# Which of three PSUM banks the soft-max may use, and when the first float16 attention tiles are given out

## The chip, the cores and the metric

The kernel runs on one core of a Trainium2 chip. A core has TensorE (PE, matrix products, with its weight loads shown apart as PEld), VectorE (DVE), ScalarE (ACT), GpSimd (POOL) and SyncE (SP), which here only issues transfers. Each works through its own list of instructions in order, and semaphores make one wait for another. PE writes into PSUM banks, which DVE and ACT read. The metric is the device time of one execution in microseconds (us); smaller is better.

## The reference

Attention within chunks of 64 positions, then a mixture layer with squared ReLU, then a soft mixture over 32 slots. Cut to what matters:

```python
scores = scale * q_c @ k_c^T            # 8 batches, 8 heads, 9 chunks of 64 x 64
attn = softmax(scores, axis=-1)
x = (attn @ v_c) -> rows                # 4608 tokens x 512
h = maximum(x @ w_in, 0.0)              # 512 -> 2048
x = (h * h) @ w_out                     # 2048 -> 512
logits = x @ phi                        # 4608 x 32
d = softmax over the tokens (axis 0);  slot_input = d.T @ x
slot_out[e] = maximum(slot_input[e] @ w1[e], 0.0) @ w2[e]      # 8 experts
out = softmax over the slots (axis 1) of logits @ slot_out
```

## The kernel before, in words

**Tiles and blocks.** The tokens are cut into 36 attention tiles of 128 rows. Tiles 0 to 8 are computed in float32 (`attention32`), tiles 9 to 35 as pairs of float16 values (`attention`). Tiles are grouped into blocks of three (the first two blocks are smaller). For a block, the squared-ReLU layer runs as 16 steps, one for each 128 of the 2048 hidden columns: a step is 12 matmuls into the buffer `hps` (line 780), a ReLU and a square on ACT, and for most steps a transpose `gT` on PE (815) that ACT copies away (213). After the 16 steps of block b the generator `soft(b)` updates a running soft-max over all tokens, one stage to a step: the logits `L` are scaled to `Ls` (980), PE spreads them into a bank `l4` (990), DVE takes the maximum (1000, 1001) and ACT the exponential `dts` (1004), PE turns the logits (949) and the exponentials (1018), and PE multiplies the exponentials by the hidden values into `y` (1068), which DVE adds to `acc` (1052).

**One float16 tile, in order.** `total` (207: largest values), `flip`, `top`, `spread`, `scale` (420, 425, 429, 240: one scale for v), `reduce`, `finish` (230, 240, 243: scales for q and k), `hi` on ACT (446), `lo` on DVE (451), the transposing DMA `T` into `qkT` (472), `qd` (476), the scores `qk` on PE (487 to 489), `max` and `less` on DVE (493, 496), `exp` on ACT (502), `sums` on DVE (507 to 509), `normal` on POOL (512), `phi` on ACT (522), `plo` on POOL (525), the transposing DMA `PT` into `pT` (528), `pv` on PE (539 to 541), `xh` (545), `xl` (551). Parallel to it `vh` on POOL (461) and `vl` on DVE (466) fill `vbd`. Buffers go by the parity of the tile number; those of the first float16 tiles are made anew (`zero`, 181 and 182) once the float32 tile of the same parity has done its `pv` (708).

**What sets the order.** Up to the end of the float32 tiles a planner (`list_schedule`) writes the order out. After that a loop over steps t does, in each step: it gives out the operations of the tiles that are due (`put_until`, `put`), then the step's 12 matmuls, ReLU and square, then the stages of the soft-max that are due, then the transpose of the step two before. Each operation of a tile has a stage number, which is compared with the step (`FIRST` for tiles 9 to 11, `STAGES` from tile `FULL` = 12 on). `put` holds one back until what it depends on has been given out, and by `behind` some steps earlier: at least one step for PE behind another engine, two or three behind a DMA. From step `ALL_FROM` = 23 on the code's order holds on PE, DVE, ACT and POOL; before that only on PE, and a scheduler orders the others.

**The banks.** Three PSUM banks, `misc0` to `misc2`, serve all of the small PE work: `reduce`, `flip`, `spread`, `qk`, `pv` and the soft-max. `misc()` gives them out in turn and passes over a bank that is in `held_banks`: there a tile's operation is entered, when it is given out, with the operations that read it (`gives`), and it stays until these are given out too. The soft-max calls `misc()` without such an entry. Whoever writes into a bank waits, by semaphore, until those who read its last contents are done.

Of the kernel before, what the change touches and what calls it, by code (L numbers as in the profile page):

```python
# [20 lines left out]
P = 128  # L21
# [19 lines left out]
FULL = 12  # L41
# [44 lines left out]
def kernel(  # L86
# [25 lines left out]
    dve, act, pool, pe, sp = nc.vector, nc.scalar, nc.gpsimd, nc.tensor, nc.sync  # L112
# [77 lines left out]
    ps_h = ps1.enter_context(tc.tile_pool(name="ps_h", bufs=2, space=PSUM))  # L190
    ps_m = ps1.enter_context(tc.tile_pool(name="ps_m", bufs=1, space=PSUM))
    bank_of, n_misc, turn, held_banks = {}, [0], [None], {}

    def misc():
        x = bank_of.get(turn[0])
        if x is None:
            while n_misc[0] % 3 in held_banks:
                n_misc[0] += 1
            x = n_misc[0] % 3
            n_misc[0] += 1  # L200
            if turn[0] is not None:
                bank_of[turn[0]] = x
        return ps_m.tile([P, 512], F32, tag=f"misc{x}", name="misc")
# [734 lines left out]
    def late_keep(x, eng):  # L938
        moe_keep(NB - 1, NF - LATE + x, eng)
# [35 lines left out]
    def soft(b):  # L975
        nonlocal cmat
        s0, n = blocks[NB if b == 1 else b]
        L, iv = L_ps.pop(b), iv2_all[:, s0 : s0 + n]
        Ls = big.tile([P, 4, P], F32, tag="Ls", name="Ls")[:, :n]
        dve.tensor_tensor(  # L980
            out=Ls, in0=L[:, : n * P].rearrange("p (j t) -> p j t", j=n),
            in1=iv.unsqueeze(2).to_broadcast([P, n, P]), op=ALU.mult,
        )
        if b == 2:
            second_gT[0] = True
        yield
        if cmat is None:
            cmat = const.tile([P, NT, NS], F32, tag="lg", name="cmat", bufs=1)
        l4 = misc()[:, : n * P]
        pe.matmul(  # L990
            l4, sel4.rearrange("p a s -> p (a s)"), Ls.rearrange("p j t -> p (j t)"),
            start=True, stop=True,
        )
        yield
        rm = sm.tile([P, 1], F32, tag="rm", name="rm", bufs=2)
        nm = sm.tile([P, 1], F32, tag="nm", name="nm", bufs=2)
        al = sm.tile([P, 1], F32, tag="al", name="al", bufs=2)
        rsum = sm.tile([P, 1], F32, tag="rsum", name="rsum", bufs=2)
        dts = big.tile([P, 4, P], F32, tag="dts", name="dts")[:, :n]
        dve.tensor_reduce(out=rm, in_=l4, axis=AX.X, op=ALU.max)  # L1000
        dve.scalar_tensor_tensor(
            out=nm, in0=rm, scalar=-1.0, in1=run_n, op0=ALU.mult, op1=ALU.min
        )
        act.activation(  # L1004
            out=dts.rearrange("p j t -> p (j t)"), in_=l4, func=ACTF.Exp, bias=nm, accum_out=rsum
        )
        act.activation(out=al, in_=run_n, func=ACTF.Exp, bias=nm, scale=-1.0)
        dve.tensor_copy(run_n, nm)
        yield
        new_sum(al, rsum)  # L1010
        cs = slots_exp(s0, n, slots_turn(Ls, n, misc()))
        if b > 2:
            yield
        slots_share(s0, n, cs)
        yield
        tp = misc()[:, : n * NS].rearrange("p (j s) -> p j s", s=NS)
        for j in range(n):
            pe.transpose(tp[:, j], dts[:NS, j], ident[:NS, :NS])
        dd = wk.tile([P, 3, NS], F32, tag="dd", name="dd", bufs=1)[:, :n]
        parts = None  # L1020
        if b in BY_DMA:
            top, inv = (sm.tile([P, w], F32, tag=f"iv{w}", name="iv", bufs=2) for w in (1, 3))
            dve.tensor_reduce(out=top, in_=iv, axis=AX.X, op=ALU.max)
            dve.reciprocal(inv[:, :1], top)
            dve.tensor_scalar(inv, iv, inv[:, :1], 8.0, ALU.mult, ALU.mult)
            pool.tensor_scalar(
                out=top, in0=top, scalar1=0.125, scalar2=1.0, op0=ALU.mult, op1=ALU.mult
            )
            act.activation(out=acc, in_=acc, func=ACTF.Copy, scale=al)
            iv = inv  # L1030
        dve.tensor_tensor(  # L1031
            out=dd, in0=tp, in1=iv.unsqueeze(2).to_broadcast([P, n, NS]), op=ALU.mult
        )
        if b in BY_DMA:
            parts = aux_of()[1].rearrange("p (l j s) -> p l j s", l=6, j=3)[:, 3 * (b % 2) : 3 * (b % 2) + 3]
            dve.tensor_scalar_mul(parts[:, 0], dd, 4096.0)
            dve.scalar_tensor_tensor(
                out=parts[:, 1], in0=dd, scalar=4096.0, in1=parts[:, 0],
                op0=ALU.mult, op1=ALU.subtract,
            )  # L1040
            dve.tensor_scalar_mul(parts[:, 2], parts[:, 0], 2.0 ** -12)
        if b > 2:
            yield
        y = misc()
        for j in range(n):
            slot_sums(b, y, dd, j, n, parts)
        if b in BY_DMA:
            dve.scalar_tensor_tensor(
                out=acc, in0=y, scalar=top, in1=acc, op0=ALU.mult, op1=ALU.add
            )  # L1050
        else:
            dve.scalar_tensor_tensor(
                out=acc, in0=acc, scalar=al, in1=y, op0=ALU.mult, op1=ALU.add
            )
        yield
# [253 lines left out]
    convs = {f: conv(f) for f in range(NF)}  # L1309
    emitted = set()  # L1310

    def emit(task, name, op):
        emitted.add((task, name))
        turn[0] = (task, name)
        op()
        turn[0] = None
        if (task, name) in bank_of:
            held_banks[bank_of[task, name]] = [(task, n) for n in gives[name]]
        for x, users in list(held_banks.items()):
            if all(u in emitted for u in users):  # L1320
                del held_banks[x]


    fa, fb = PARTS
# [218 lines left out]
    for i in range(9, NT):  # L1543
        b, j = tile_block[i]
# [7 lines left out]
    def behind(t, op, d):  # L1552

        eng = tiles[d[0][1]][d[1]].eng if d[0][0] == "t" else ""
        gap = (3 if op.eng == "pe" else 2) if eng == "dma" else op.eng == "pe" and eng != "pe"
        return t - placed.get(d, -99) >= gap

    def put(i, stage, t):
        whole = True
        for n, op in tiles[i].items():  # L1560
            me = ("t", i)
            if op.stage <= stage and (me, n) not in emitted:
                full = len(held_banks) == 3 and op.eng == "pe"
                if not full and all(
                    d in emitted and behind(t, op, d)
                    for d in (d if isinstance(d, tuple) else (me, d) for d in op.deps)
                ):
                    placed[me, n] = t
                    emit(me, n, op)
                else:  # L1570
                    whole = False
        return whole
# [58 lines left out]
    t = min(0, min(slots, default=0))  # L1631
# [2 lines left out]
    )  # L1634
    while t < end or any(x >= t for x in slots):
        if t == ALL_FROM:
            ctx.enter_context(
                tc.manual_schedule(engines={getattr(mybir.EngineType, e) for e in ALL})
            )
        put_rest(t)  # L1640
        put_until(t + 1)
        b, f = steps[t] if 0 <= t < len(steps) else (None, None)
        if b == 2 and f % QF == 0:
            put_rest(t, [("s", NB, x) for x in range(f, f + QF)])
        if b is not None:
            end_step = (b, f) == (NB - 1, NF - 1)
            moe_h(b, f)
            moe_relu(b, f)
            if end_step:
                late_turn(0)  # L1650
                late_keep(0, "dve")
            if by_dma(b, f):
                moe_parts(b, f)
            else:
                moe_square(b, f)
            if (b, f) == (NB - 1, NF - 1):
                give((big, f"xb{b % 2}", 1536))
        if 1 <= t <= len(steps) and by_dma(*steps[t - 1]):
            moe_rest(*steps[t - 1])
        for fn in slots.pop(t, []):  # L1660
            fn()
        if b == NB - 1 and f % 2:
            give((big, f"wi{f // 2}", 1024))
        if 0 <= t - LAG < len(steps):
            b, f = steps[t - LAG]
            if (b, f) < (NB - 1, NF - LATE) and not by_dma(b, f):
                moe_turn(b, f)
                moe_keep(b, f)
            if f % QF == QF - 1 and (b, f) != (NB - 1, NF - 1):
                moe_logits(b, f // QF)  # L1670
            if f == NF - 1:
                if b < NB - 1:
                    run_gen(t + 1, soft(b))
                else:
                    soft_last()
        t += 1
# [212 lines left out]
```

## Time and profile before

| | |
|---|---|
| median of 3 runs | 775.44 us (771.95 to 776.62) |
| the profiled execution | 771.75 us |
| its span, first to last instruction | 770.0 us |
| PE busy in the span | 694.6 us, 90% |
| DVE, ACT, POOL busy | 499.5, 467.7, 196.8 us |
| mean granted clock of PE | 0.976 of full speed |

A busy share says how long an engine had work under way. An engine that is busy throughout sets the time; where it idles, the row of its wait tells who released it. The page also cuts the span into 40 slices of 19.25 us.

### The profile page before, as it was taken

The numbers are of one execution on the slowest core, as the hardware profiler recorded it, in microseconds if no ns is written. First come the engines' busy times: TensorE is split into PE (matmuls) and PEld (weight loads), VectorE is DVE, ScalarE is ACT, GpSimd is POOL, SyncE is SP. The second block draws the span as 40 slices with busy tenths as digits, with TensorE's granted clock in tenths as the row PEclk, the third lists the DMA queues.
The fourth block names the chain that finished last, engine by engine and source line by source line (L and its number), as shares of the span: only waits on it lengthen the run. The fifth ranks groups of instructions, "written<-read, shape, count | busy, mean of one in ns | idle before, by whom it ended". The sixth has DMA issues, their size and how long they took to land.

```text
span 770.0 us, 16709 instructions
## 1 busy us (share of the span) xinstructions
PE 694.6 (90%) x6491; PEld 437.8 (57%) x6491; DVE 499.5 (65%) x1108; ACT 467.7 (61%) x954; POOL 196.8 (26%) x250
## 2 busy tenths in 40 slices
PE   4688999888399899999999999999999999999983
PEld 3577776655256556555565565655655656553342
DVE  4899996256644778887778787777877741123134
ACT  3688887663446567667576675766766765541133
POOL 3222211122213335444333132232322310002010
PEclk9899999999799999999999999999999999999988
DMA  7796833214605746678577686785776976478979
GB/s 156 218 268 175 219 122 123 52 36 107 137 15 97 124 101 126 123 132 155 104 128 124 122 160 115 135 129 105 152 124 129 244 213 184 131 286 333 385 262 345
DMA packets 280655, 123.06 MB, mean 160 GB/s; under 512 B 251648, under 2 KB 268032, under 8 KB 280576
## 3 DMA queue, kind: packets, MB, share of 16 engines
q1 hardware_dynamic: 280576, 122.00, 66.8%
q8 instruction: 51, 0.84, 0.5%
q14 instruction: 28, 0.23, 0.1%
HBM read 78.71 MB, written 9.44 MB: 114 GB/s over the span
## 4 chain that ended last, share of the span: by engine, by line
PE 64%; DVE 19%; DMA 8%; ACT 3%; issue 3%; POOL 1%; SPq 1%; DVEq 0%; POOLq 0%; ACTq 0%
PE hps L780 36%; PE gT L815 4%; PE misc L1068 4%; PE L L866 4%; DMA qkv<-in_q_dram 3%; DMA qkv<-in_v_dram 2%; DVE qk L301 2%; DVE am L207 2%; PE ehps L1720 2%; DVE vbd L466 2%; DVE parts L847 1%; DVE qk L451 1%; DMA unit<-in_moe_w_dram 1%; DMA qkT<-qk 1%; PE misc L487 1%
## 5 line engine op out<-in xcount | busy, mean ns | idle before, releaser
L780 PE MATMUL hps<-xb,wi 128*128 128x384 f16 (+2 forms) x2400 | 409.6, 321 | 0.0
L780 PEld LDWEIGHTS <-wi 128*128 128x128 f16 x2400 | 222.3, 98 | 141.0 <-issue 20.1
L796 ACT ACTIVATE g<-hps 128x384 f32<-128x384 f32 x144 | 70.8, 491 | 125.7 <-PE hps L780 125.1
L803 ACT ACTIVATE g<-g 128x384 f32<-128x384 f32 (+2 forms) x188 | 96.9, 515 | 5.2
L213 ACT ACTIVATE G<-gT 128x384 f32<-128x384 f32 (+2 forms) x128 | 58.8, 459 | 23.5 <-PE gT L815 12.4
L207 DVE TENSOR_REDUCE am<-qkv 128x1 bf16<-128x512 f32 x90 | 59.1, 678 | 19.5 <-DMA qkv<-in_v_dram 11.3
L815 PE MATMUL gT<-ident,g 128*128 128x128 f32 x372 | 63.8, 278 | 2.5 <-ACT G L213 2.5
L525 POOL TENSOR_TENSOR p<-ex,p 128x512 f16<-128x512 f32 x27 | 34.3, 1271 | 116.4 <-ACT p L522 116.4
L815 PEld LDWEIGHTS gT<-ident,g 128*128 128x128 f32 x372 | 46.3, 143 | 20.7 <-issue 9.8
L461 POOL TENSOR_SCALAR vbd<-qkv,avs 64x512 f16<-64x512 f32 x54 | 47.0, 871 | 39.7 <-DVE vbd L181 20.1
L466 DVE SCALAR_TENSOR_TENSOR vbd<-qkv,avs,vbd 64x512 f16<-64x512 f32 x54 | 45.7, 846 | 2.9 <-POOL vbd L461 2.1
L796 ACT ACTIVATE g<-hps,inv_w 128x384 f32<-128x384 f32 (+2 forms) x56 | 29.9, 533 | 27.3 <-PE hps L780 25.5
L451 DVE SCALAR_TENSOR_TENSOR qk<-qkv,as,qk 128x512 f16<-128x512 f32 x54 | 44.8, 869 | 0.8 <-ACT qk L446 0.8
L248 POOL TENSOR_SCALAR iv_all<-avi 128x1 f32<-128x1 f32 x27 | 14.7, 544 | 111.5 <-DVE avi L243 109.4
L866 PE MATMUL L<-g,wp 128*32 128x384 f32 x384 | 41.9, 498 | 0.0
L512 POOL TENSOR_TENSOR ex<-ex,rs 128x512 f32<-128x512 f32 x27 | 30.6, 1133 | 40.8 <-DVE es L439 15.6
L847 DVE SCALAR_TENSOR_TENSOR parts<-parts,g 128x384 f16<-128x384 f16 x64 | 35.7, 557 | 7.3 <-ACT g L803 6.6
L446 ACT ACTIVATE qk<-qkv,as 128x512 f16<-128x512 f32 x54 | 35.7, 709 | 4.1 <-DVE as L240 4.1
L841 ACT ACTIVATE parts<-g 128x384 f16<-128x384 f32 x64 | 33.5, 523 | 2.0
L1068 PE MATMUL misc<-G,dd 128*32 128x512 f32 x180 | 33.5, 596 | 1.1 <-DVE dd L1031 1.1
L487 PE MATMUL misc<-qkT,qbd 128*128 128x64 f16 x216 | 21.9, 194 | 13.4 <-ACT dts L1004 13.4
L539 PE MATMUL misc<-pT,vbd 128*128 128x64 f16 x216 | 22.3, 195 | 10.5 <-DMA pT<-p 10.5
(213 smaller groups left out, 1166.5 us busy)
## 6 DMA issues: line engine op xcount, KB each, us to landing
unit<-in_moe_w_dram SPq DMA_DIRECT2D x49, 512.0 KB, 6.5
qkv<-in_q_dram SPq DMA_DIRECT2D x72, 128.0 KB, 3.2
qkv<-in_k_dram SPq DMA_DIRECT2D x72, 128.0 KB, 3.5
qkv<-in_v_dram SPq DMA_DIRECT2D x72, 128.0 KB, 3.4
stage<-in_moe_w_in_dram SPq DMA_DIRECT2D x16, 512.0 KB, 5.1
stage<-in_moe_w_out_dram SPq DMA_DIRECT2D x16, 512.0 KB, 6.2
unit<-in_moe_w_dram SPq DMA_DIRECT2D x27, 256.0 KB, 6.9
out_dram<-o SPq DMA_DIRECT2D x20, 256.0 KB, 2.8
```

The costliest lines, as they stand in the source:

```text
L207: dve.tensor_reduce(out=am, in_=src, axis=AX.X, op=ALU.max, apply_absolute_value=True)
L213: act.activation(out=out, in_=in_, func=ACTF.Copy)
L451: dve.scalar_tensor_tensor(out=qk16[:, 2 * a + 1], in0=flat[:, a], scalar=v["s"][:, a : a + 1], in1=qk16[:, 2 * a], op0=ALU.mult, op1=ALU. ...
L461: pool.tensor_scalar(out=dst[0], in0=vin, scalar1=v["sv"][pr], scalar2=1.0, op0=ALU.mult, op1=ALU.mult,)
L466: dve.scalar_tensor_tensor(out=dst[1], in0=vin, scalar=v["sv"][pr], in1=dst[0], op0=ALU.mult, op1=ALU.subtract,)
L780: pe.matmul(hp, wi[f][:, wl, kt], xb[:, xl, kt], start=(nm == 0), stop=(nm == 3 * KT - 1))
L796: act.activation(out=g, in_=hp, func=ACTF.Relu, scale=sc)
L803: act.activation(out=g, in_=g, func=ACTF.Square)
L815: pe.transpose(gt_ps[b, f][:, j], g[:, j * P : (j + 1) * P], ident)
L847: dve.scalar_tensor_tensor(out=part[:, 1], in0=part[:, 0], scalar=-4096.0, in1=g, op0=ALU.mult, op1=ALU.add)
L866: pe.matmul(L_ps[g0][NS * x : NS * x + NS, :n], wp[:, QF * q + x], g[:, x, :n], start=(q == 0), stop=(q == NQ - 1), tile_position=(0, NS * x),
L1068: pe.matmul(y[NS * g : NS * g + NS], lhs, rhs, start=(j == 0 and x == 0), stop=(j == n - 1 and last), tile_position=(0, NS * g), skip_grou ...
```

## The change

There are three edits.

1. A bank taken for the soft-max's `l4` is entered in `held_banks` under the name ("soft", b), and `let_go` takes it out after the stage that reads it has been written (`keep`). This holds from step 23 on.
2. From step 23 on `misc()` gives out, of the banks that are not held, the one that was taken or let go longest ago, in place of the next in turn.
3. In `put`, tiles below `FULL` (9 to 11) no longer ask `behind`, nor whether all three banks are held: what they depend on must have been given out, and their stage number must have come.

```diff
-    def misc():
+    last_use, by_age = {0: 0, 1: 0, 2: 0}, [False]
+
+    def used(x):
+        n_misc[0] += 1
+        last_use[x] = n_misc[0]
+
+    def misc(keep=None):
         x = bank_of.get(turn[0])
-        if x is None:
-            while n_misc[0] % 3 in held_banks:
+        if x is None and by_age[0]:
+            x = min((y for y in last_use if y not in held_banks), key=last_use.get)
+            used(x)
+            if turn[0] is not None:
+                bank_of[turn[0]] = x
+            if keep is not None:
+                held_banks[x] = [keep]
+        elif x is None:
+            while len(held_banks) < 3 and n_misc[0] % 3 in held_banks:
                 n_misc[0] += 1
...
-        l4 = misc()[:, : n * P]
+        l4 = misc(("soft", b))[:, : n * P]
...
         dve.tensor_copy(run_n, nm)
+        let_go(("soft", b))
         yield
...
+    def let_go(*done):
+        emitted.update(done)
+        for x, users in list(held_banks.items()):
+            if all(u in emitted for u in users):
+                del held_banks[x]
+                if by_age[0]:
+                    used(x)
...
-                full = len(held_banks) == 3 and op.eng == "pe"
+                full = len(held_banks) == 3 and op.eng == "pe" and i >= FULL
                 if not full and all(
-                    d in emitted and behind(t, op, d)
+                    d in emitted and (i < FULL or behind(t, op, d))
...
         if t == ALL_FROM:
+            by_age[0] = True
```

The instructions are the same in kind and number. The lines of the changed kernel lie 12 or 13 lower (487 becomes 499, 949 becomes 961).

**Place 1: the first float16 scores.** PE, behind the last float32 `pv` (708, then 720), before:

```order
L708 MATMUL misc<-pT,vbd 64x64 x16
L420 LDWEIGHTS am
L420 MATMUL misc<-aux,am 1x128
L780 LDWEIGHTS wi_1780
L780 MATMUL hps<-xb_86,wi_1780 128x384
```

And there in the changed kernel:

```order
L720 MATMUL misc<-pT,vbd 64x64 x16
L499 LDWEIGHTS qbd
L499 MATMUL misc<-qkT,qbd 128x64
L500 LDWEIGHTS qbd
L500 MATMUL misc<-qkT,qbd 128x64
L501 LDWEIGHTS qbd
L501 MATMUL misc<-qkT,qbd 128x64
...
L432 LDWEIGHTS am
L432 MATMUL misc<-aux,am 1x128
```

The 24 matmuls of tile 9's scores now stand directly behind that `pv`; before, three steps of 12 matmuls lay between. Its `pv` moves up by one step.

**Place 2: tile 9's way to its `pT`.** ACT between the exponential of tile 9's scores (`ex_83`) and its `phi` (`p_85`), before:

```order
L502 ACTIVATE ex_83<-ex_83,es 128x512
L796 ACTIVATE g<-hps,inv_w 128x384
L213 ACTIVATE G<-gT 128x3x128
L803 ACTIVATE g<-g 128x384
...
L213 ACTIVATE G<-gT 128x3x128
L446 ACTIVATE qk_80<-qkv_78,as 128x512 x2
L1004 ACTIVATE dts,rsum<-misc,nm 128x384
L522 ACTIVATE p_85<-ex_83 128x512
```

In the changed kernel:

```order
L514 ACTIVATE ex_83<-ex_83,es 128x512
L808 ACTIVATE g<-hps,inv_w 128x384
L225 ACTIVATE G<-gT 128x3x128
L815 ACTIVATE g<-g 128x384
L808 ACTIVATE g<-hps,inv_w 128x384
L225 ACTIVATE G<-gT 128x3x128
L534 ACTIVATE p_85<-ex_83 128x512
L815 ACTIVATE g<-g 128x384
L458 ACTIVATE qk_81<-qkv_79,as 128x512 x2
```

SP there, before (`p_85` is tile 9's, `p_84` tile 10's):

```order
L391 DMA qkv_79<-in_q_dram 64x8x64 x2
L472 DMA_TRANSPOSE qkT<-qk_81 128x16x128
L391 DMA qkv_79<-in_k_dram 64x8x64 x2
L391 DMA qkv_78<-in_q_dram 64x8x64 x2
L472 DMA_TRANSPOSE qkT<-qk_80 128x16x128
L528 DMA_TRANSPOSE pT<-p_85 128x8x128
L528 DMA_TRANSPOSE pT<-p_84 128x8x128
```

In the changed kernel:

```order
L403 DMA qkv_78<-in_v_dram 64x8x64 x2
L540 DMA_TRANSPOSE pT<-p_85 128x8x128
L403 DMA qkv_79<-in_q_dram 64x8x64
L484 DMA_TRANSPOSE qkT<-qk_81 128x16x128
L403 DMA qkv_79<-in_q_dram 64x8x64
L403 DMA qkv_79<-in_k_dram 64x8x64 x2
L540 DMA_TRANSPOSE pT<-p_84 128x8x128
```

On both engines tile 9's step now stands ahead of the `hi` and the `T` of tile 11 (and, on SP, of tile 12's), behind which it stood before.

**Place 3: the scores behind a soft-max bank.** PE at step 45, tile 17, with the engines each waits for, before:

```order
L420 MATMUL misc_4065<-aux_2066,am_3698 1x128 [waits DVE_49]
L487 LDWEIGHTS qbd_2317 [waits DMAHW6_49,DVE_49]
L487 MATMUL misc_4069<-qkT_2319,qbd_2317 128x64 [waits Activation_49]
L488 LDWEIGHTS qbd_2317
...
L780 MATMUL hps_4097<-xb1_87,wi2_920 128x384
L949 MATMUL misc_4113<-sel1_67,Ls_3969 128x32 [waits DVE_49]
```

In the changed kernel:

```order
L432 MATMUL misc_4065<-aux_1994,am_3698 1x128 [waits DVE_49]
L499 LDWEIGHTS qbd_2317 [waits DMAHW6_49,DVE_49]
L499 MATMUL misc_4069<-qkT_2319,qbd_2317 128x64 [waits DVE_49]
L500 LDWEIGHTS qbd_2317
...
L792 MATMUL hps_4097<-xb1_87,wi2_920 128x384 [waits Activation_49]
L961 MATMUL misc_4113<-sel1_67,Ls_3969 128x32 [waits Activation_49]
```

No instruction moves here: the scores got another bank, and the soft-max's own bank goes to its next matmuls (949), behind the step's 12.

## Rows read from the trace of the kernel before

**Rows 1.** The page: busy time of PE; granted clock in 40 slices, tenths

```profile
PE 694.6 (90%) x6491; PEld 437.8 (57%) x6491; DVE 499.5 (65%) x1108; ACT 467.7 (61%) x954; POOL 196.8 (26%) x250
PEclk9899999999799999999999999999999999999988
```

**Rows 2.** One stretch: length, then PE, PEld, DVE, ACT, POOL busy; clock; DMA

```profile
308.00:385.00 77.00, 73.42 (x693) 44.68 (x691) 62.01 (x145) 51.16 (x104) 31.77 (x37) 1.00 0.70 129
```

**Rows 3.** Waits of PE, 154 to 280 us: total, times, longest

```profile
PE misc L539 <- DMA pT<-p: 10.5, 1, 10.5
PE misc L429 <- DVE xb L719: 2.7, 1, 2.7
PE misc L487 <- ACT dts L1004: 2.7, 1, 2.7
PE misc L230 <- DVE ex L496: 1.3, 1, 1.3
```

**Rows 4.** Waits of PE, 280 to 640 us

```profile
PE misc L487 <- ACT dts L1004: 10.7, 6, 1.8
```

**Rows 5.** Timeline of PE, 160 to 235 us: start, length, instruction

```profile
175.80 1.15 PE L708 MATMUL misc<-pT,vbd 128*64 128x64 f32 x32
...
187.73 0.20 PE L487 MATMUL misc<-qkT,qbd 128*128 128x64 f16 x1
...
209.05 0.21 PE L539 MATMUL misc<-pT,vbd 128*128 128x64 f16 x1 [10.53 <-DMA pT<-p]
...
210.42 0.18 PE L429 MATMUL misc<-tm,ones 1*128 1x1 bf16 x1
...
210.58 3.98 PE L780 MATMUL hps<-xb,wi 128*128 128x384 f16 x12
```

**Rows 6.** Timeline of PE, 255 to 270 us

```profile
264.62 0.19 PE L487 MATMUL misc<-qkT,qbd 128*128 128x64 f16 x1 [2.68 <-ACT dts L1004]
...
265.32 3.77 PE L780 MATMUL hps<-xb,wi 128*128 128x384 f16 x12
```

**Rows 7.** Timeline of PE, 305 to 322 us

```profile
315.78 0.19 PE L487 MATMUL misc<-qkT,qbd 128*128 128x64 f16 x1 [1.79 <-ACT dts L1004]
...
316.48 2.11 PE L780 MATMUL hps<-xb,wi 128*128 128x384 f16 x12
```

**Rows 8.** Timeline of all engines, 196 to 206 us

```profile
196.76 1.04 POOL L512 TENSOR_TENSOR ex<-ex,rs 128x512 f32<-128x512 f32 x1 [8.03 <-ACT ex L502]
...
198.41 1.34 ACT L446 ACTIVATE qk<-qkv,as 128x512 f16<-128x512 f32 x2 [1.31 <-DVE as L240]
...
200.21 0.62 ACT L522 ACTIVATE p<-ex 128x512 f16<-128x512 f32 x1
200.28 2.32 DVE L451 SCALAR_TENSOR_TENSOR qk<-qkv,as,qk 128x512 f16<-128x512 f32 x2
...
200.90 1.15 POOL L525 TENSOR_TENSOR p<-ex,p 128x512 f16<-128x512 f32 x1 [3.10 <-ACT p L522]
...
202.66 2.88 SPq L472 DMA_TRANSPOSE qkT<-qk  x1
...
205.64 1.25 SPq L528 DMA_TRANSPOSE pT<-p  x1
```

**Rows 9.** Timeline of DVE, 150 to 212 us

```profile
174.83 0.86 DVE L476 COPY qbd<-qkT 64x1024 f16<-64x1024 f16 x2 [2.37 <-DMA qkT<-qk]
175.70 0.75 DVE L1052 SCALAR_TENSOR_TENSOR acc<-acc,al,misc 128x512 f32<-128x512 f32 x1
...
182.02 2.46 DVE L207 TENSOR_REDUCE am<-qkv 128x1 bf16<-128x512 f32 x4
```

**Rows 10.** Line 451 in the whole trace: shortest, median, longest in ns

```profile
L451 DVE SCALAR_TENSOR_TENSOR qk<-qkv,as,qk x54: 699/751/1655, 167.9 to 601.1; 128x512 f16<-128x512 f32 x54
```

**Rows 11.** Timeline of all engines, 313 to 318 us

```profile
313.18 0.15 DVE L243 TENSOR_SCALAR ai<-misc 128x2 int32<-128x2 int32 x1
...
315.06 0.58 ACT L1004 ACTIVATE dts<-misc,nm 128x384 f32<-128x384 f32 x1
```

More of the change, by code (lines that the diff above doesn't have):

```diff
@@ L1318, in emit @@
             held_banks[bank_of[task, name]] = [(task, n) for n in gives[name]]
-        for x, users in list(held_banks.items()):
-            if all(u in emitted for u in users):
-                del held_banks[x]
+        let_go()
     fa, fb = PARTS
```

## The prediction

> **What bounds the kernel now.** I read the page first, then stretches of 77 us, then the waits of PE, and last the timelines around the longest of them. The page has PE busy for 90% of the span, with the granted clock at full level but for the slices at both ends and one at 192 to 212 us, where it shows 7 tenths [rows 1]. In the middle PE is the bound: of 77.00 us it works 73.42 [rows 2], and the 3.58 us left are two waits of 1.79 us. So there a microsecond of PE's waiting taken away is a microsecond of the span, as long as DVE (62.01 of 77.00) and ACT (51.16) can follow.
>
> The waits name two causes. Between 154 and 280 us one wait of 10.5 us for `pT` stands out, with three of 2.7, 2.7 and 1.3 us [rows 3]. From 280 to 640 us there is a single kind: six waits of 1.8 us, 10.7 us in all, in which the scores of a tile wait for ACT's exponential of the soft-max [rows 4]. One of the 2.7 us waits is of this kind too. Scores need nothing of the soft-max; they wait because they were given the bank that holds `l4`.
>
> The timeline shows what a wait costs beyond itself. Tile 9's `pv` starts at 209.05 us after 10.53 us of idle time, and the next 12 matmuls take 3.98 us [rows 5]. Behind the 2.68 us wait at 264.62 the same 12 take 3.77 us [rows 6]; behind a 1.79 us wait they take 2.11 [rows 7]. So two of these stalls put the clock on its lower level (1.2 in place of 2.4 GHz) for a step, and the shown 1.79 us one does not.
>
> **Part A, the kept bank and banks by age (step 23 on).** No instruction moves. The seven scores no longer wait for the exponential (place 3): 10.7 + 2.7 = 13.4 us [rows 3, 4]. With the wait at 264.62 goes its slow step, 3.77 - 2.11 = 1.66 us [rows 6, 7]. What is late next: the scores take the bank of the `reduce` one step earlier, read by DVE's line 243, which ends at 313.33; without the stall the scores could start at 315.78 - 1.79 = 313.99, so 0.66 us are left [rows 7, 11]. The wait for the exponential passes to the soft-max's turn (949), behind 0.70 us of scores (315.78 to 316.48) and a step of 12 matmuls; the exponential ends at 315.64, and the turn would come at about 313.99 + 0.70 + 1.95 = 316.64, with 1.95 us as my estimate of a step's 2.11 without its overlap with the next [rows 7, 11]. That is 1.0 us of cover; after the longer wait at 264.62, whose exponential is 0.9 us later against PE, it is nearly nothing. I leave 0.3 us for that. Taking the oldest bank elsewhere only renames banks whose readers are two or more steps back: nothing, hidden by those steps; if they were one step back, it would be the 0.66 us case again. Sum of part A: -13.4 - 1.66 + 0.3 = **-14.8 us**. Bounds: 0, if another wait takes each place, and -15.1.
>
> **Part B, tiles 9 to 11 by stage number alone.** Tile 9's scores move up three steps (place 1), its `pv` one step, and its way to `pT` is shorter (place 2). Gone are, if `pT` is in time: the wait of 10.53 us; the slow step behind it, 3.98 - 2.11 = 1.87; and the slow `pv` itself, 209.05 to 210.42 = 1.37 us against 0.70 for 24 matmuls of the same form in rows 7: 0.67 [rows 5, 7]. The `spread` of tile 10 waited 2.7 us because the scale of the last float32 tile (line 719) was late behind DVE's queue; now 24 matmuls and a whole step lie ahead of it, so 2.7 go [rows 3]. Sum -15.8.
>
> Is `pT` in time? Before, the scores started at 187.73 and `pT` landed at 209.05, 21.3 us later [rows 5]. Now the scores start behind the last float32 `pv`: at 175.80 + 1.15, and 1.3 more for a new wait (below), so at 178.2. PE came to the old `pv` at 209.05 - 10.53 = 198.5, 22.7 us after 175.80. Take from these the waits of 2.7 and 1.3 (the latter now lies behind it) and one step with its transposes (2.5, my estimate from the 2.11 of rows 7) and add the new 1.3: PE comes to the new `pv` at 193.3. If the way still takes 21.3 us, `pT` lands at 199.5 and PE waits 6.2 us, with another slow step of 1.87. But part of the way was queueing. `normal` ended at 197.80, and `phi` started at 200.21, behind tile 11's `hi` on ACT, which itself waited for its scale: 2.4 us. `plo` ended at 202.05, and SP issued `pT` at 205.64, behind tile 11's transpose: 3.6 us [rows 8]. Both now stand behind it. 21.3 - 2.4 - 3.6 = 15.3, so `pT` lands at about 193.5, just as PE comes. I take 0.5 us of wait, and 0 to 6.2 as its bounds.
>
> New costs of part B. The last float32 `pv` (708) now takes the bank of `y`, which DVE reads at line 1052. DVE comes to it behind line 476, whose end, 174.83 + 0.86, hangs on a DMA, and in the new order behind one more reduction; with 0.7 us for that (my estimate, from the shortest line 451, which reads as many elements) and 0.75 for 1052 it ends at about 177.1, while `pv` could start at 175.80: +1.3 us [rows 5, 9, 10]. Two `lo` in place of one stand ahead of the bank read that line 697 waits for: at most one of 0.75, half of it absorbed by the wait behind it, +0.4 [rows 10]. The 1.3 us wait of `reduce` stays, with another cause: tile 12's `reduce` now has the bank of the second block's `l4`, which is not kept before step 23, and waits for its exponential [rows 3]: 0. Tile 9's `hi`, now earlier on ACT, delays float32 work that has a step of cover: 0, and up to 1.34 if that cover were gone [rows 8]. Sum of part B: -15.8 + 0.5 + 1.3 + 0.4 = **-13.6 us**. Bounds: -15.8 and, with `pT` 6.2 us late, the slow step and the 1.34, -4.7.
>
> **The sum.** The last part of the program (weights of the experts, output) is released by steps, not by the clock, so it moves up as a whole. 771.75 - 14.8 - 13.6 = 743.4 us against the profiled execution, which is 3.7 us (0.5%) below the median of 775.44. Scaled by that, 743.4 x 775.44 / 771.75 = 746.9; I say **746 us**, since the profiled execution and the lowest of the three lie together at 772.
>
> One rule of the Trainium skill would make part A larger. The rows give back a slow step for one stall in two shown. "TensorE: Matmul & The Clock Gate", section "A second HAM failure mode: psum-queue depth-cycling", says that a kernel which cycles through PSUM banks idles in small gaps often enough for the clock to swing between its levels. By that each of the six short stalls would give back some 1.66 us more, 10 us in all, and the sum would be 736. The 2.11 us step in rows 7 speaks against it here.
>
> **The rivals.**
>
> *`pT` comes late all the same.* For it: the landing and PE's arrival are level by my sum, and DVE and POOL slow each other down: two `lo` took 2.32 us while POOL worked, against 0.75 us for the median one, and up to 1.66 [rows 8, 10]. Against it: 6.0 us of queueing are gone. Time: 746 + 6.2 + 1.9 - 0.5 = 754, to 757 with further DVE delay.
>
> The skill names such a sharing: "GPSIMD Engine Reference", section "1. Specifications", has the engine's memory interfaces shared with VectorE, with contention where an instruction of VectorE reads two inputs from SBUF. Rows 8 and 10 agree. It speaks against moving tile 9's POOL steps next to other tiles' `lo` and `vl`.
>
> *The stalls of part A only change hands.* The scores wait for DVE's line 243, or the turn (949) for the exponential. For it: 0.66 and 1.0 us of slack are small, and DVE reads its way through a long queue. Against it: DVE works 81% of that stretch, and regains a microsecond within a step or two. Time: 746 + 14.8 = 761.
>
> *Slower than before.* With one of three banks kept for two steps, all else goes through two; if DVE falls behind by more than the 0.66 us of rows 11 and stays behind, PE waits in each of the nine rounds of the soft-max behind step 23. It decides from the point at which such a wait is long enough to take the clock down, as the 2.68 us one did: 2.68 + 1.66 = 4.3 us a round, 39 us in nine, in place of the 15.1 that part A would remove: 746 + 14.8 + 39 - 15.1 = 785. Against it stands the 19% of the time in which DVE is idle there [rows 2].
>
> *It does not do what it says.* If the scheduler of ACT and DVE put the moved work so that PE waits as long elsewhere, and part A were lost too, the time stays at 770 to 777. The new order of place 2 makes that unlikely.
>
> **How the numbers follow.** Forecast, both parts within their sums, 739 to 751: 0.65. `pT` late, 751 to 758: 0.17. Part A changes hands, 756 to 764: 0.08. Not done, 768 to 777: 0.04. Slower: 0.03. By the clock rule, or otherwise below 738: 0.03. The range of 738 to 759 takes in the first two but for their tails and half of the third, about 8 in 10. About 1% is what a measurement of this kernel can tell from no change; faster by more than that (below 767.7) is 0.65 + 0.17 + 0.08 + 0.03 = 0.93, the same 0.04, slower 0.03.
>
> **What would show it.** In the profile of the changed kernel, the waits of PE from 280 us on should have no row of scores behind the exponential (now on line 499 and 1016), and stretches of 77 us in the middle should have PE busy for 76 us and more. The wait for `pT` should be gone or below 2 us, the 12 matmuls behind it at 2.1 us, and the clock's slices should show 9 throughout the middle. A short wait of the last float32 `pv` (720) for DVE should appear near 176 us. I am wrong if scores then wait for DVE for a microsecond or more, if `pT` keeps PE waiting for over 5 us, or if the end part, from the last step to the last output, gets longer than it was.

## The result, and the profile after

The changed kernel takes 750.6 us (median of 4 runs, 744.96 to 750.93) against 776.0: ratio 0.967, 95% interval 0.961 to 0.972. In a later comparison (e11, below) it was 0.972, 0.970 to 0.975. The profiled execution of it took 750.67 us, 21.1 less than that of the kernel before; the prediction's sum was 28.4 less. The kernel before was measured at 776.0, 772.9, 775.5, 774.3 and 773.5 us in the five comparisons of this document; the ratio, for which the two ran side by side, is the safer number.

The page of the changed kernel, busy time of PE and granted clock by slices:

```profile
PE 695.4 (93%) x6491; PEld 439.2 (59%) x6491; DVE 499.9 (67%) x1108; ACT 467.1 (62%) x954; POOL 197.4 (26%) x250
PEclk9999999999999999999999999999999999999987
```

PE works as long as before [rows 1] in a shorter span, and the slice of 7 tenths in the middle is gone (the last slice, at the program's end, is now at 7). Its waits, first from 154 to 280 us, then from 280 to 640 us:

```profile
PE misc L1081 <- DVE dd L1044: 3.9, 2, 2.4
PE misc L242 <- ACT dts L1016: 1.8, 1, 1.8
PE misc L709 <- DVE cmat L972: 1.3, 1, 1.3
PE misc L720 <- ACT pT L225: 1.2, 1, 1.2
PE misc L441 <- DVE xb L563: 1.1, 1, 1.1
PE misc L720 <- DVE acc L1065: 1.0, 1, 1.0
...
PE misc L499 <- DVE qbd L488: 1.0, 1, 1.0
```

The seven waits of the scores for the exponential [rows 3, 4] are gone, and one of 1.0 us for `qd`'s copy has come. The wait for `pT` is gone too. In its place stand short waits that the list of before has not, or has shorter (only that of line 720 for `pT` was there, with the same 1.2 us); `dd` for the slot sums (1081) is the largest. In the middle PE is now busy for 76.03 of 77.00 us, against 73.42 [rows 2]:

```profile
308.00:385.00 77.00, 76.03 (x718) 45.87 (x716) 63.34 (x141) 53.72 (x109) 32.26 (x37) 1.00 0.73 127
```

Place 3, at the round of [rows 7, 11], all engines:

```profile
302.31 0.20 PE L499 MATMUL misc<-qkT,qbd 128*128 128x64 f16 x1
...
303.02 2.11 PE L792 MATMUL hps<-xb,wi 128*128 128x384 f16 x12
...
303.46 0.58 ACT L1016 ACTIVATE dts<-misc,nm 128x384 f32<-128x384 f32 x1
...
304.97 0.75 PE L961 MATMUL misc<-sel,Ls 128*128 128x32 f32 x6
```

The scores start before the exponential has begun, and the turn (961) comes 0.93 us after its end at 304.04: the forecast had 1.0 us of cover there. The places on PE where time went between 150 and 215 us:

```profile
156.05 3.28 PE L792 MATMUL hps<-xb,wi 128*128 128x384 f16 x12
...
174.94 2.78 PE L1081 MATMUL misc<-G,dd 128*32 128x512 f32 x24 [1.55 <-DVE dd L1044]
...
195.17 0.19 PE L551 MATMUL misc<-pT,vbd 128*128 128x64 f16 x1
...
197.94 0.16 PE L242 MATMUL misc<-am,ones 128*128 128x2 bf16 x1 [1.76 <-ACT dts L1016]
...
198.00 2.11 PE L792 MATMUL hps<-xb,wi 128*128 128x384 f16 x12
...
201.51 0.17 PE L441 MATMUL misc<-tm,ones 1*128 1x1 bf16 x1 [1.08 <-DVE xb L563]
...
201.66 2.11 PE L792 MATMUL hps<-xb,wi 128*128 128x384 f16 x12
...
210.21 4.17 PE L1081 MATMUL misc<-G,dd 128*32 128x512 f32 x24 [2.36 <-DVE dd L1044]
```

Tile 9's `pv` (551) starts at 195.17 us without a wait, and the two steps behind it (198.00 and 201.66) take 2.11 us each. But 15 us later PE waits 2.36 us for `dd`, and the 24 slot sums behind that wait take 4.17 us where the first ones took 2.78. DVE just ahead of it:

```profile
196.86 0.23 DVE L437 TENSOR_REDUCE tm<-misc 1x1 bf16<-1x128 f32 x1
199.60 1.14 DVE L488 COPY qbd<-qkT 64x1024 f16<-64x1024 f16 x2 [2.51 <-DMA qkT<-qk]
200.77 0.69 DVE L563 SCALAR_TENSOR_TENSOR xb<-misc,xb 128x512 f16<-128x512 f32 x1
...
207.15 0.26 DVE L971 TENSOR_REDUCE cm<-misc 128x3 f32<-128x96 f32 x1
...
209.01 0.85 DVE L488 COPY qbd<-qkT 64x1024 f16<-64x1024 f16 x2
209.90 0.26 DVE L1044 TENSOR_TENSOR dd<-misc,iv_all 128x96 f32<-128x96 f32 x1
```

DVE idles 2.51 us at tile 11's `qd`, and tile 9's `xl` (563), whose input from ACT was there at 197.33, stands behind it. Then `cm` starts at 207.15, though PE had turned the logits at 203.60 to 204.35, and one more `qd` stands ahead of `dd`.

**Where the 21.1 us came from.** The same step of 12 matmuls can be found in both traces, and the difference of its starts is what has been gained by then: 0.3 us at 148 us, 7.4 from 215 on (222.09 before, 214.70 after), 10.0 at the step of the first round (265.32 before), which was slow, 11.6 behind it, and 1.85 more at each of the next six rounds, less 1.0 for the new wait at 384.7: 21.63 at the last steps. The end part is 0.5 us longer here: its waits for expert weights (line 1824) are 3.36 in place of 2.79 us. In e11, the same kernel again, it is 1.2 us shorter than before, so this is what one execution differs from the next by. So part A gave 21.63 - 7.39 = 14.2 us and part B 7.39 - 0.34 = 7.05 (0.34 was there ahead of any change).

### The profile page after: what moved, and what is told of

It reads as the page before. It is cut to its first block, busy times and chain, and to the rows that moved or that the text cites. A ratio compares the mean times of both kernels' runs of the same rounds, so it can differ in the third digit from the quotient of the medians.

```text
span 748.9 us, 16702 instructions
## 1 busy us (share of the span) xinstructions
PE 695.4 (93%) x6491; PEld 439.2 (59%) x6491; DVE 499.9 (67%) x1108; ACT 467.1 (62%) x954; POOL 197.4 (26%) x250
## 4 chain that ended last, share of the span: by engine, by line
PE 74%; DVE 12%; DMA 7%; ACT 2%; issue 1%; SPq 1%; POOL 1%; POOLq 0%; DVEq 0%; ACTq 0%
PE hps L792 44%; PE gT L827 5%; PE L L878 4%; PE misc L1081 4%; DMA unit<-in_moe_w_dram 2%; DVE qk L313 2%; DMA qkT<-qk 2%; DMA qkv<-in_q_dram 2%; PE ehps L1740 1%; PE misc L499 1%; PE ops L1807 1%; DVE qk L312 1%; DVE stage L318 1%; DMA qkv<-in_v_dram 1%; PE misc L500 1%
## 5 line engine op out<-in xcount | busy, mean ns | idle before, releaser
L488 DVE COPY qbd<-qkT 64x1024 f16<-64x1024 f16 x54 | 24.4, 451 | 8.4 <-DMA qkT<-qk 8.1
L505 DVE TENSOR_REDUCE mx<-misc 128x8 f32<-128x512 f32 x27 | 18.4, 682 | 11.2 <-PE misc L501 11.2
```

## The experiments

Diffs are against the changed kernel.

**e1: the banks alone.** Edit 3 is taken back.

```diff
-                full = len(held_banks) == 3 and op.eng == "pe" and i >= FULL
+                full = len(held_banks) == 3 and op.eng == "pe"
...
-                    d in emitted and (i < FULL or behind(t, op, d))
+                    d in emitted and behind(t, op, d)
```

> Edits 1 and 2 (kept bank, banks by age) without edit 3: tiles 9 to 11 ask `behind` and the count of held banks again. Theory Q (the two parts add up; what part B lacks was lost in DVE's queue ahead of step 23): the seven waits of scores for the exponential go with one slow step, 14.2 us by the positions of the steps in the two traces, so 776.0 - 14.2 = about 762 us; the 10.5 us wait for pT is there again, and no wait of line 487's scores for ACT from 280 us on. Rival I (the banks cost part B its missing 6.6 us): alone they give less or more than 14.2, and the 6.6 us turn up in edit 3 alone: 764 to 766 here. Rival H (the gain of part A is not in these waits): no change, 776.

760.0 us, ratio 0.983 (0.979 to 0.987). No wait of PE stands in the list from 280 to 640 us, and from 308 to 385 us it is busy throughout. The wait for `pT` is back. One stretch, and one row of the waits from 154 to 280 us:

```profile
308.00:385.00 77.00, 77.00 (x735) 46.89 (x733) 63.92 (x149) 53.45 (x109) 32.62 (x37) 1.00 0.75 136
```

```profile
PE misc L551 <- DMA pT<-p: 12.6, 1, 12.6
```

1.7% of 773 is 13 us (10 to 16 by the interval), as theory Q and part A's sum have it.

**e2: edit 3 alone.** Banks go in turn throughout.

```diff
         if t == ALL_FROM:
-            by_age[0] = True
```

> Edit 3 without edits 1 and 2: banks in turn throughout, l4 not kept. PE's order is that of the changed kernel. Theory Q: -7.0 us as the steps' positions show, 776.0 - 7.0 = 769 us, with PE's waits for dd of 1.5 and 2.4 us (line 1081) and the slow multiplication of 4.2 us behind the second as in the changed kernel, and the seven waits of the scores for the exponential back. Rival I: no waits for dd, and the whole 13.6 us that were forecast for this part: 762 us.

765.0 us, 0.990 (0.986 to 0.994): 7.9 us. The waits for `dd` are there without the banks' edits, and the exponential's are back, as the rows below show. The two ratios multiplied give 0.973, where both together measured 0.967 and 0.972, so the parts add up. The time of e2 alone would not decide, as it lies between the 769 of theory Q and the 762 of rival I; the waits for `dd`, which rival I had gone, and the 13 us of e1 do. What part B lacks is part B's own.

```profile
PE misc L1081 <- DVE dd L1044: 3.5, 2, 2.5
...
PE misc L499 <- ACT dts L1016: 10.7, 6, 1.8
```

**e3: kept, but in turn.** No banks by age; `l4` is entered as held in the rotation too.

```diff
             x = n_misc[0] % 3
             n_misc[0] += 1
+            if keep is not None and keep[1] > 2:
+                held_banks[x] = [keep]
...
-            by_age[0] = True
```

> As the changed kernel, but banks are given out in turn throughout; l4's bank is kept from the third block's soft-max on. My theory now: keeping alone gives nothing, because l4's readers are written at step 44 of the round at place 3, which lets the bank go, and the turn comes to this very bank for the scores at step 45, whose wait for the exponential is as long as before. So the time of edit 3 alone: 769 us, with the waits of scores for ACT of some 1.8 us each. Rival (keeping is what removes the wait, age is dressing): as the changed kernel, 751 us, no such waits.

766.7 us, 0.991 (0.988 to 0.994): that is edit 3 alone. Keeping the bank by itself gives nothing:

```profile
PE misc L501 <- ACT dts L1018: 10.8, 6, 1.8
```

**e4: by age, not kept.**

```diff
-        l4 = misc(("soft", b))[:, : n * P]
+        l4 = misc()[:, : n * P]
```

> As the changed kernel, but l4 is taken without a name, so its bank is never entered as held; banks by age from step 23 on. My theory now: the scores no longer get l4's bank, but the `flip` (line 432) that stands directly before them does, since l4's is the oldest then; the wait of 1.8 us passes from the scores to the flip, and the time is that of edit 3 alone, 769 us, with six or seven waits of line 432 for ACT. Rival (age alone is enough): as the changed kernel, 751 us.

778.3 us, 1.004 (1.001 to 1.008). The wait passed to the `flip` (432), as expected, but the time is 13 us above that of edit 3 alone. The waits are a little longer, and PE's steps behind them are slow. Waits from 280 to 640 us, then the timeline of one, then two stretches of 12 us:

```profile
PE misc L432 <- ACT dts L1016: 11.6, 6, 1.9
```

```profile
311.88 0.22 PE L432 MATMUL misc<-aux,am 128*1 128x128 bf16 x1 [1.94 <-ACT dts L1016]
...
313.27 3.22 PE L792 MATMUL hps<-xb,wi 128*128 128x384 f16 x12
```

```profile
308.00:320.00 12.00, 10.06 (x79) 6.13 (x78) 7.19 (x23) 6.42 (x14) 3.74 (x5) 0.86 0.58 109
412.00:424.00 12.00, 10.07 (x90) 6.17 (x87) 8.76 (x26) 7.22 (x16) 4.56 (x5) 1.00 0.58 110
```

Behind five of the six waits of 1.94 us the granted clock fell to its lower level for a while (0.86 over the 12 us), and the step behind took 3.2 to 3.8 us in place of 2.11: 6.8 us in all (17.39 - 5 x 2.11). Behind the sixth (415.26 us) it did not. Behind the six of 1.79 us, before and in e2 and e3, it never did. That makes 9.3 us with the 0.9 by which the six waits are longer and a seventh wait of 1.55 us (line 499, at 618 us); the two profiled executions, e4's and e2's, drift apart by 10.7 us from the first round of the soft-max to the last, and by 3.4 ahead of step 23, where the two kernels are alike.

Which bank each user gets at place 3, as the code gives them out (the bank that `l4` had is in bold where it is taken next):

| step, user | before | e3: kept, in turn | e4: by age | changed |
|---|---|---|---|---|
| 43, `l4` | 0 | 2 | 1 | 0 |
| 44, reduce | 1 | 0 | 2 | 1 |
| 45, flip | 2 | 1 | **1** | 2 |
| 45, scores | **0** | **2** | 0 | 1 |
| 45, turn (961) | 1 | 0 | 2 | **0** |

`l4`'s readers are written at step 44, so at 45 the bank is free in the code's eyes, though the exponential has yet to run. What keeps the scores off it is that being let go counts as a use: it makes `l4`'s bank the youngest. That takes both edits.

**e5: the slot sums a step later**, to see whether taking away the waits for `dd` gives their length back.

```diff
-        if b > 2:
-            yield
+        yield
         y = misc()
```

> The changed kernel, with the slot sums (`y`, line 1081) of the first two soft-maxes written one step later, as those from the third block on are. PE then has 12 matmuls, a transpose and, in the first, the last float32 pv and tile 9's scores ahead of the matmuls that need dd. Theory Q (what part B lacks is dd, late behind other work on DVE): the waits of 1.55 and 2.36 us for dd go, and with the second the slow multiplication (4.17 instead of 2.78 us), and the 1.02 us of the last float32 pv for the read of y's bank: 1.55 + 2.36 + 1.39 + 1.02 = 6.3 us, 750.6 - 6.3 = 744 us; with the next late thing at half of the first wait, 746. Rival L (DVE as a whole is late there, so whatever PE does next waits as long): the waits turn up at other lines between 170 and 225 us, 750 us.

752.1 us, 0.969 (0.967 to 0.971): nothing gained. Rival L held. The waits (140 to 235 us) moved:

```profile
PE misc L242 <- ACT dts L1016: 4.9, 1, 4.9
...
PE misc L1080 <- DVE ex L508: 2.7, 1, 2.7
PE misc L709 <- DVE cmat L972: 2.7, 1, 2.7
```

**e6: kept ahead of step 23 too.**

```diff
             x = n_misc[0] % 3
             n_misc[0] += 1
+            if keep is not None:
+                held_banks[x] = [keep]
```

> The changed kernel, with l4's bank also kept in the first two soft-maxes, ahead of step 23 (banks in turn there). Tile 12's reduce no longer gets l4's bank of the second block, and tile 11's spread no longer that of tile 9's pv: the waits of 1.76 us (line 242 for the exponential) and 1.08 us (line 441 for DVE's line 563) go, 750.6 - 2.8 = 748 us. Rival L: PE waits as long at the next thing that comes out of DVE (the dd wait of 2.36 us gets longer by 2.8): 750 us.

754.1 us, 0.972 (0.970 to 0.975): no gain again. Tile 12's reduce no longer waits for the exponential; it waits for tile 9's `xl`, three times as long:

```profile
PE misc L244 <- DVE xb L565: 5.3, 1, 5.3
```

**e7: both.**

> Both of the last two edits on the changed kernel. Theory Q: the sum of their gains, 6.3 + 2.8 = 9.1 us, 741.5 us, or 743 if one of them is partly given back to the next late thing; between 154 and 225 us only the waits for G (2.3), pT (1.2) and cmat (1.3) are left. Rival L: 748 to 750 us.

754.0 us, 0.970 (0.966 to 0.975). Theory Q, here that the waits for `dd` are a cost of their own, falls: whatever PE asks of DVE there comes late. The question became whether DVE has too much to do, or does it in a bad order. It is busy for 48.39 of the 77 us from 154 on, so the order was tried.

**e8: code order from step 13.** DVE, ACT and POOL keep the order of the code ten steps earlier. DVE then has tile 9's `xl` ahead of tile 11's `qd`, and `dd` ahead of tile 11's `vl`.

```diff
-        if t == ALL_FROM:
-            by_age[0] = True
+        by_age[0] = t >= ALL_FROM
+        if t == 13:
```

> The changed kernel, but DVE, ACT and POOL run in the order of the code from step 13 on, not from 23 (banks by age still from 23). DVE then has tile 9's xl ahead of tile 11's qd, for whose transposed tile it idled 2.51 us in the changed kernel, and the soft-max's chain to dd ahead of tile 11's vl. Theory O (new: it is the order on DVE between 195 and 212 us that keeps PE waiting, not its amount of work): the wait of line 441 (1.08) goes, that for dd (2.36, and 1.39 of slow matmuls behind it) shrinks below 1 us, line 242's 1.76 for the exponential stays: 750.6 - 1.1 - 3 = 746 to 747 us. Rival W (DVE has too much to do in that stretch, so any order leaves PE waiting): the waits turn up at other lines, 750 us or more.

748.9 us, 0.968 (0.964 to 0.972): between what theory O and rival W had, and by the ratio not to be told from the changed kernel. The wait of line 441 is gone and the second one for `dd` is down from 2.36 to 0.35 us; a slow step of 4.04 us at 173.94, behind a wait of 2.60 us for `cmat`, where the order is still the scheduler's, took part of it back.

**e9: the same with `l4` kept throughout** (the edits of e6 and e8).

> As the run before, and l4's bank kept in the first two soft-maxes too. Kept alone, this passed the wait of line 242 from the exponential to tile 9's xl (5.3 us), which now stands ahead of the qd. Theory O: that wait is below 1 us, and the others as in the run before: 746.5 - 1.5 = 745 us. Rival W: 750 us or more, with a wait of some 5 us of line 242 for xl.

748.4 us, 0.967 (0.962 to 0.973), again between the two forecasts. The wait of line 242 for `xl` is 1.27 us here, where it was 5.3 without the code's order.

**e10: edit 3 for PE alone.** The other engines' operations of tiles 9 to 11 ask `behind` again, which puts tile 9's scores at step 10 instead of 8.

```diff
-                    d in emitted and (i < FULL or behind(t, op, d))
+                    d in emitted and (i < FULL and op.eng == "pe" or behind(t, op, d))
```

> The changed kernel with edit 3 for PE's operations alone: DVE's, ACT's, POOL's and the transfers of tiles 9 to 11 ask `behind` again. Tile 9's reduce is given out at step 6 in place of 4 (7 before the change), its scores at step 10 in place of 8 (11 before); pv stays at 13. In the changed kernel pT was issued 10.8 us behind the first score and took some 3.1 us to land; with scores two steps later, near 185.4 us, it lands near 199.3, and PE comes to pv at 195.2 at the latest: a wait of 4 us or more and a slow step behind it. Theory of the prediction (pT's landing decides): slower than the changed kernel by 4 to 6 us, 755 us, less what the wait hides of those behind it (3.7 us for dd): 751 to 756. Rival (the early scores crowd DVE, and later ones relieve it by more): 747 us.

753.6 us, 0.975 (0.971 to 0.979), within the 751 to 756 that the prediction's theory has, though the changed kernel's interval in e11 (0.970 to 0.975) overlaps, so the time does not decide. The waits do: `pT` is late by 6.6 us, and the second wait for `dd` is down from 2.36 to 0.4 us. My reading is that the time in which PE stands for `pT` lets DVE catch up, as in the kernel before, where that wait was 0.35 us:

```profile
PE misc L551 <- DMA pT<-p: 6.6, 1, 6.6
PE misc L1081 <- DVE dd L1044: 2.3, 2, 1.9
```

**e11 and e12: the changed kernel and that of e9 side by side**, five rounds on one chip.

> The changed kernel unaltered, beside the next run on one chip, so that the two can be compared: 750.6 us as before. Its profile tells which waits between 150 and 215 us come again (the dd waits of some 1.5 and 2.4 us with 1.4 of slow matmuls should) and which change from execution to execution (the slow step at 156 us may).

> Code order from step 13 with l4 kept throughout, again. Theory O (the order on DVE cost what part B lacked there): by the waits of its last profile the dd wait of the second soft-max with its slow matmuls (2.0 + 1.4) and line 441's 1.1 are gone and some 0.9 us of a new wait for qd are added: 3 to 4 us below the changed kernel in the same call, 747 us. Rival W (what one order gives another takes): within 1 us of the changed kernel.

752.2 us, 0.972 (0.970 to 0.975), against 746.7 us, 0.966 (0.964 to 0.969): 5.5 us between the medians, and the intervals lie just apart. Where the difference comes from can be read off the starts of the same two steps, first in e11, then in e12:

```profile
185.05 2.12 PE L792 MATMUL hps<-xb,wi 128*128 128x384 f16 x12
...
218.72 2.11 PE L792 MATMUL hps<-xb,wi 128*128 128x384 f16 x12
```

```profile
183.49 2.12 PE L794 MATMUL hps<-xb,wi 128*128 128x384 f16 x12
...
211.91 2.11 PE L794 MATMUL hps<-xb,wi 128*128 128x384 f16 x12
```

e12 is 1.6 us ahead at the first of them, before step 13, and 6.8 at the second; a new wait of 0.9 us for a `qd` (238.8) gives some of it back, and 6.0 are left at the last steps. So the new order is worth 4.4 us. The same reading gives 4.2 us for e8 (against e11) and 4.2 for e9 (against the changed kernel's first profile), all of it gained between the same two steps. So theory O holds, and e12 beats the changed kernel too. In e11 the waits for `dd` and the slow sums came again (4.42 us behind a wait of 2.44). Of e12, PE's waits from 140 to 235 us, then DVE at the place that was shown of the changed kernel:

```profile
PE misc L711 <- DVE cmat L974: 2.9, 1, 2.9
...
PE misc L244 <- DVE xb L565: 1.3, 1, 1.3
...
PE misc L1083 <- DVE dd L1046: 0.7, 2, 0.4
```

```profile
198.94 0.69 DVE L565 SCALAR_TENSOR_TENSOR xb<-misc,xb 128x512 f16<-128x512 f32 x1 [0.21 <-ACT xb L559]
...
206.78 0.85 DVE L490 COPY qbd<-qkT 64x1024 f16<-64x1024 f16 x2
208.50 0.26 DVE L1046 TENSOR_TENSOR dd<-misc,iv_all 128x96 f32<-128x96 f32 x1 [0.87 <-PE misc L1033]
```

DVE no longer idles at the `qd`, and at `dd` it waits 0.87 us for PE, where PE's own wait is 0.35. e8, e9 and e12 change the order on ACT and POOL as well; that it is DVE's which counts is read off these rows, not tested alone.

## Why the prediction was right, and where it was off

The sign and the range held; the time came out 4.6 us above the forecast of 746 (6.2 in e11). That it lies within 739 to 751, the forecast for both parts within their sums, is luck by 0.4 us, since part B gave about half of its sum: by the profiled executions 21.1 of the 28.4 us came.

- **Part A, -14.8: measured -14.2.** Each of the six short waits gave 1.85 us, the long one with its slow step 4.2; what was left over for the next late thing was 1.0 us (one wait for `qd`, fed by a DMA) instead of 0.3. The 0.66 us of slack for the scores and the 1.0 us for the turn were enough, so the rival that they change hands did not come. What the prediction did not ask is which of the two edits does it. It took banks by age for a renaming elsewhere; e3 and e4 show that neither edit is worth anything without the other.
- **Part B, what it removes, 15.8: measured 15.7**. The wait of 10.53 us, the slow step behind it (1.87) and the 2.68 us of `spread` are gone, and the `pv` takes 0.80 us in place of 1.37.
- **`pT` in time: right.** PE came to `pv` at 195.2 us, not 193.3, and `pT`, issued at 191.13 and 3.0 to 3.1 us on its way, had been there for about 1 us. From the first score (180.30) that is 13.9 us in place of the 15.3 of the forecast. e10 shows how near it was: with the scores two steps later PE waits 6.6 us, about the upper bound that the prediction gave (6.2).
- **The new costs named, 2.2 with `pT`'s 0.5: measured 2.1.** 1.02 us for `y`'s bank (1.3 forecast), 0.66 more at line 709 (0.4), 0.45 more at `reduce` (0).
- **The new costs not named: 6.5 us.** This is the step that failed. The sum of part B went through PE's order and let DVE follow; its premise, "as long as DVE (62.01 of 77.00) and ACT (51.16) can follow", was looked at for the middle only, and by busy share. Before, PE stood still for 10.5 us, in which DVE caught up; with the stall gone PE comes earlier to everything behind it, and DVE, working in a fixed order with a `qd` that waits for a transposing DMA, does not. It cost 2.0 us more for the second `dd` (2.36, and 0.35 before), 1.4 for the slow sums behind it, 0.8 more for the first `dd` (1.55, and 0.71 before), and 1.1 for `xl`: 5.3 us. The other 1.2 us are a slow step at 156 us, which e12 has not and e11 has; it comes with some executions of the same code, so it is no cost of the change. So part B gave 15.7 - 2.1 - 6.5 = 7.1 us (7.05 by the positions), not 13.6; without that slow step it would be 8.2, near the 7.9 of e2. The prediction's bound of -4.7 held, but by another mechanism.
- **The signs of being wrong.** The end part was 0.5 us longer in this execution and 1.2 us shorter in e11's, so this sign says nothing. Scores waiting for DVE for a microsecond or more came to 0.97 us, once (384.7): DVE was late with a `qd`, for which it had itself waited 1.50 us for a transposing DMA.
- **The clock rule** of the Trainium skill ("TensorE: Matmul & The Clock Gate", section "A second HAM failure mode: psum-queue depth-cycling") would have made the sum 736. For this change the trace differs: the 1.79 us waits gave back no slow steps. In e4, with waits of 1.94 us, the trace agrees with it, five times of six.
- **The price of a long stall.** The prediction took one stall of 2.68 us with its slow step as the measure for a kernel that gets slower. The trace of before has a second wait of 2.68 us, and the step behind it was not slow (last section), so that price was not a sure one.

A rule of the Trainium skill stands beside e3: "Perfetto Trace Analysis", section "Matmuls", has independent matmul groups rotate through different PSUM banks so that one's evacuation overlaps the next one's matmuls. No run contradicts it, but e3 rotates, and PE waits 10.8 us. Who read the bank last, and when, has to be in the choice.

What stays open: e8 and e9 can't be told apart (0.968 and 0.967), and which of the changes in the order is worth most, on DVE or on ACT and POOL, was not tried. Why the clock falls near 157 us in some executions and not in others, and what decides it behind stalls of about the same length, was not found.

## What to carry to other kernels

When a long stall goes, ask not only what the stalled engine meets next, but who caught up during the stall. Here that engine was late at one meeting point after the other, and taking those waits away one at a time (e5 to e7) passed them on. Look instead at the order of the late engine, above all for an instruction that waits for a DMA ahead of one that could run (e8, e12). And a buffer is free when its last reader has run, not when it has been written in the code, so keep it entered until its readers are written, and then choose the one that was released longest ago; here neither was worth anything without the other (e3, e4).

## What the runs showed of the hardware

A stall's length alone did not set its price. Behind the 1.79 us waits for the exponential (six each before, in e2 and in e3) the next step took 2.11 us each time; behind e4's of 1.94 us, which stand before the `flip` just ahead of the scores, it took 3.2 to 3.8 us five times of six. But e4's wait of 1.99 us at 201.1 us was followed by 2.11, and so was a wait of 2.68 us in the kernel before, as long as the one at 264.62 that was followed by 3.77 [rows 6]:

```profile
182.16 0.17 PE L429 MATMUL misc<-tm,ones 1*128 1x1 bf16 x1 [2.68 <-DVE xb L719]
...
182.30 2.11 PE L780 MATMUL hps<-xb,wi 128*128 128x384 f16 x12
```

The granted clock was 1.00 from 180 to 184 us, and 0.68 from 264.6 to 270.

And the same code does not always meet the lower level at the same place: of two profiled executions of one kernel (e9, then e12), the step behind the two waits for `G` near 155 us took

```profile
158.42 3.83 PE L794 MATMUL hps<-xb,wi 128*128 128x384 f16 x12
```

```profile
157.09 2.11 PE L794 MATMUL hps<-xb,wi 128*128 128x384 f16 x12
```

behind waits of 1.76 and 0.73 us in the one and 1.77 and 0.74 in the other.
